# A four-layer network on one core: how the modes' parts of a long-convolution kernel are split and loaded, and where the first layer's norm is computed

## The chip, the cores and the metric

The kernel runs on one core of one Trainium2 chip. A core has five engines that run side by side, each with its own queue of instructions: TensorE (PE: products; PEld: the loading of their weights), VectorE (DVE), ScalarE (ACT), GpSimd (POOL), and SyncE (SP), which here issues nearly all of the DMAs. The metric is the device time of one execution in microseconds (us). Times are compared by the median of several runs; the profile is of one execution.

## The reference

The input is a matrix x of 2048 positions by 512 channels. Four residual layers follow one another, A, B, A, B, and each takes a layer norm over the channels first:

```
x = x + A(layernorm(x));  x = x + B(layernorm(x))      # twice
A(x) = irfft2(rfft2(x) * (w_r + i w_i))                # 2048 x 512, a spectral filter
B(u) = irfft(rfft(u, 4096) * rfft(K, 4096))[:2048] + u * D_skip
K[d, l] = 2 Re sum_n C[d, n] exp(A[d, n] dt[d] l)      # 128 modes n for each channel d
A[d, n] = -exp(log_A_real) + i A_imag;  C = (C_real + i C_imag) dt;  dt = exp(log_dt)
```

K, the kernel in time, does not depend on x; both B layers use the same one. The norm subtracts the mean of a row and divides by the root of its variance.

## The kernel before

Transforms are done as products with tables of cosines and sines, in steps that TensorE can do. Three strands matter here.

**The first layer A** has three stages. *Spread* (`layer_a.spread`, 16 steps) loads rows of x, takes their norm and transforms along the positions. *Middle* (18 steps) transforms along the channels, weighs with w and goes back. *End* (`end`, 19 steps) consists of `fold` (lines 565 to 590: products, a copy on ScalarE, an addition and a subtraction on VectorE, and additions on GpSimd that give the tile wv) and, three steps later, of `rows_back` (592 to 614): a product gives 128x512 values of one row per partition, the residual row hr is loaded from x, VectorE adds the product to it (601), and the sum is stored to DRAM (603), where the next layer reads it. When a group of rows is complete (`LN`, here groups of 4, 4, 4, 2, 1, 1 rows), `layer_norm_stats` computes two numbers for each row, scale and offset, into `norms`: statistics per row (339), their aggregation (340), and a chain of small VectorE operations per group, an inverse square root by three Newton steps (345 to 362).

**The modes of the second layer's K.** `kernel_parts` computes five numbers per mode and channel into the tile val (called V; raw, tmp and val are its working tiles): logarithm and phase of the start, decay, and two phases. `kernel_parts` is a generator: each `yield` ends one of its ten steps, which are put in between the first layer's spread steps (1123). At the end (769 to 775) it splits the 128x2560 values of all four blocks of channels into three bf16 parts that add up to them: a cast on ScalarE (771), a subtraction on VectorE (773), and a store to the DRAM tensor parts for each part.

**The kernel in time** (`kernel_time`) runs 32 units, eight for each block of channels, in groups of four. For every second unit, `chunk` (788) loads the parts of 32 rows into the tile th, with six DMAs of 48 partitions: a slot holds two of the five numbers, one in partitions 0 to 47 and the other in 48 to 95. `grow` (804) makes magnitudes (products with the table kb at 825, exponentials, a GpSimd product); `bend`, `sine`, `cosine`, `terms` (857 to 859) and `total` (870) make the sums over the modes. Their steps are put in between the steps of the first layer's middle and end and of the second layer, by fixed shares (`FILL`).

The program is written as one list of steps, interleaved as described. A scheduler places each instruction into its engine's queue ahead of time, by the order of the program and a model of when inputs and buffers are ready; on the chip every engine then runs its own queue in that order. Tiles of one tag share a fixed number of buffers, and a new tile waits for the last user of the old one. In the first layer the tags o, f, wv and junk all draw on the seven buffers of w, and hr on the four of wt. The phase k, with kb and th, reuses the space of phase m, with raw, val, tmp and hp (the bf16 parts).

Of the kernel before, what the change touches and what calls it, by code (L numbers as in the profile page):

```python
# [32 lines left out]
WT = 4  # L33
WA = 7
LN = '444211'
PK = 2
PV = 1
# [22 lines left out]
KP = 0  # L60
S1 = 0
S2 = 0
S3 = 0
# [183 lines left out]
class Net:  # L247
# [135 lines left out]
    def layer_a(self, w, x=None, src=None, dst=None):  # L383
# [178 lines left out]
        done = []  # L562
        sizes = [int(c) for c in reversed(LN)]

# [27 lines left out]
        def rows_back(n2):  # L592
            old = row(n2, self.sb("hr", [512])) if x is None else x[:, n2]
            p = self.ps("p3", [512])
            nc.tensor.matmul(p, vs["tat"][:, n2], vs.pop(n2), start=True, stop=True)
            if not done:
                norm["sums"] = self.sb("lsum", [4], 2)
            if S2 if x is None else S3:
                self.add_up(old, old, p, norm["sums"][:, len(done):len(done) + 1])
            else:  # L600
                nc.vector.tensor_add(old, old, p)
            if x is None:
                self.dma("D")(dst[:, n2], old)
            done.append(old)
            if len(done) == sizes[-1]:
                sizes.pop()
                n = len(done)
                nr = self.layer_norm_stats(done, newton=x is None or NW[2] == "1", sums=norm["sums"][:, :n] if (S2 if x is None else S3) else None,
                                           nr=self.norms[:, :, n2 - n + 1:n2 + 1] if x is None else None)
                if x is not None:  # L610
                    for i in range(n):
                        nc.scalar.activation(self.xn[:, n2 - n + 1 + i], done[i], ACT.Identity,
                                             bias=nr[:, 0, i:i + 1], scale=nr[:, 1, i:i + 1])
                done.clear()
# [78 lines left out]
    def kernel_parts(self, kin, log_dt, parts, blks, *tags):  # L693
# [50 lines left out]
        nc.scalar.activation(mn, mn, ACT.Ln, bias=1.0)  # L744
        L = V[:, :, 2]
        D.scalar_tensor_tensor(L, e, LN2, mx, op0=ALU.mult, op1=ALU.add)
# [11 lines left out]
        D.tensor_scalar_mul(V[:, :, 0], im, -0.5)  # L758
        for c, o in ((64.0, V[:, :, 3]), (32.0, u)):
# [4 lines left out]
        D.scalar_tensor_tensor(V[:, :, 4], ph, 1 / (2 * PI), u, op0=ALU.mult, op1=ALU.add)  # L764
        yield
        self.exp(re, S[:, 2:5])
        D.scalar_tensor_tensor(V[:, :, 1], re, -1.0, dtb, op0=ALU.mult, op1=ALU.mult)
        yield
        for part in range(3):
            H = self.sb(tags[3], [n, 5, 128], dt=BF)  # L770
            nc.scalar.copy(H, V)
            if part < 2:
                D.tensor_sub(V, V, H)
            nc.sync.dma_start(parts[blks.start:blks.stop, :, part].rearrange("b q r n -> r b q n"), H)
            yield

    def kernel_time(self, parts, kt, units, group):
# [10 lines left out]
        def chunk(blk, ch):  # L788
            th = self.sb("th", [3, 2, 128], dt=BF, rows=96)
            for slot, q in enumerate((0, 1, 3)):  # L790
                for i in range(2):
                    self.dma("C")(th[48 * i:48 * i + 48, slot],
                                      parts[blk, q + i, :, 32 * ch:32 * ch + 32].rearrange("p (c h) n -> p c h n", h=2))
            state["th"] = th
# [9 lines left out]
        def grow(i):  # L804
# [9 lines left out]
            mag = self.sb("mag", [3, 512])  # L814
            for k, (slot, c) in enumerate(((0, RM), (0, RN), (1, RP))):
                if k == 1 and RNP[i % len(RNP)] != "a":
# [7 lines left out]
                p = self.ps("pk", [512])  # L824
                nc.tensor.matmul(p, th[:, slot, h], c, start=True, stop=True)
                ordered(mag[:, k], p, ACT.Exp)
            live[i] = mag, th

        def bend(i, j):
# [4 lines left out]
            p = self.ps("pk", [2, 256])  # L834
            nc.tensor.matmul(p[:, 0], th[:, 0, h], KQ[:, e], start=True, stop=False, skip_group_check=True)
            nc.tensor.matmul(p[:, 1], th[:, 2, h], KP[:, e], start=False, stop=False, skip_group_check=True)
            p = p.rearrange("p k d -> p (k d)")
# [389 lines left out]
```

## Time and profile before

| what | value |
|---|---|
| runs | 787.24, 789.84 and 782.07 us (median 787.24) |
| span of the profiled execution, first to last instruction | 781.1 us |
| its own time | not listed apart from the runs; it is at least the span |
| instructions | 18929 |
| VectorE busy | 649.3 us (83% of the span) |
| TensorE busy, products | 627.7 us (80%) |
| ScalarE busy | 428.1 us (55%) |
| GpSimd busy | 404.9 us (52%) |
| granted TensorE clock, mean | 0.934 of full speed |
| moved by DMA | 80.64 MB, mean 103 GB/s |

A row of the profile's groups reads: line, engine, operation, output tile <- input tiles, shapes and count, then busy time and mean duration of one (ns), then the idle time of the engine just before them and what ended most of it. A row of one line's instructions gives durations as min/median/max in ns and the first and last start in us. A row of the timeline gives start, duration, engine, line, operation and tiles. Busy times can overlap a wait for another engine's port, and a busy TensorE is not one at its peak.

### The profile page before, as it was taken

How to read it: one execution, taken by the hardware profiler on the slowest of the kernel's cores; microseconds unless marked ns; L12 is line 12 of the kernel's file. 1: busy time of each engine (PE TensorE's matmuls, PEld its weight loads, DVE VectorE, ACT ScalarE, POOL GpSimd, SP SyncE). 2: the span in 40 equal slices, each digit the busy share in tenths (PEclk: the TensorE clock that was granted, in tenths of full speed). 3: DMA queues.
4: the chain of work that ended last, by engine and by line, in shares of the span. 5: the costliest groups of instructions: out<-in, count | busy, mean ns of one | idle time of the engine just before them, and what ended most of it. 6: DMA issues, size and time to landing. Idle time of an engine off the chain costs nothing. (4 is left out here: it accounts for less than half of the span.)

```text
span 781.1 us, 18929 instructions
## 1 busy us (share of the span) xinstructions
PE 627.7 (80%) x7248; PEld 443.5 (57%) x7248; DVE 649.3 (83%) x1301; ACT 428.1 (55%) x919; POOL 404.9 (52%) x596
## 2 busy tenths in 40 slices
PE   3447888897867977998889887874899896989986
PEld 2336666665534543656365656654777663566766
DVE  7998748979998999769996997878578696889992
ACT  3433778854748765887568834323756336242312
POOL 3675876764825245721657266281055572475760
PEclk9998899999979997999989999997999999799998
DMA  8300552344546503452325539422133114234513
GB/s 311 128 0 1 129 138 56 110 75 151 114 167 184 137 9 64 124 145 82 51 68 117 192 55 257 141 95 69 55 82 83 28 28 136 70 95 120 154 29 83
DMA packets 144923, 80.64 MB, mean 103 GB/s; under 512 B 78561, under 2 KB 124513, under 8 KB 143937
## 3 DMA queue, kind: packets, MB, share of 16 engines
q1 hardware_dynamic: 144576, 78.90, 36.2%
q8 instruction: 58, 0.95, 0.5%
q0 software_dynamic: 256, 0.52, 0.4%
q14 instruction: 33, 0.26, 0.1%
HBM read 54.89 MB, written 25.03 MB: 102 GB/s over the span
## 5 line engine op out<-in xcount | busy, mean ns | idle before, releaser
L974 POOL TENSOR_TENSOR u<-wb,wb 64x512 f32<-64x512 f32 x90 | 129.2, 1436 | 85.2 <-DVE wb L962 75.9
L316 PE MATMUL p<-z,mb 128*64 128x512 f32 (+2 forms) x480 | 102.0, 535 | 8.3 <-DVE wb L962 5.4
L870 PE MATMUL pv<-qp 128*64 128x128 f32 x1024 | 78.9, 295 | 11.4 <-DVE qp L859 6.9
L859 DVE TENSOR_TENSOR qp<-qp,mag 128x1024 f32<-128x1024 f32 x64 | 83.8, 1317 | 1.0
L962 DVE TENSOR_TENSOR wb<-p,kk 128x512 f32<-128x512 f32 x128 | 80.6, 674 | 4.7 <-PE p L316 4.6
L870 PEld LDWEIGHTS pv<-qp 128*64 128x64 f32 x1024 | 62.0, 147 | 38.8 <-ACT stage L878 10.2
L648 ACT COPY z<-p 128x512 f32<-128x512 f32 x96 | 51.4, 597 | 58.1 <-PE p L316 43.7
L316 PE MATMUL p<-mb,u 128*64 128x64 f32 x2048 | 72.9, 235 | 10.6 <-DVE u L974 4.5
L316 PEld LDWEIGHTS p<-mb,u 128*64 128x64 f32 x2048 | 70.7, 150 | 18.7 <-issue 11.3
L857 DVE SCALAR_TENSOR_TENSOR qp<-qp,mag 128x256 f32<-128x256 f32 x128 | 64.8, 523 | 13.6 <-ACT qp L800 13.3
L654 DVE STREAM_TRANSPOSE z<-z 128x512 f32<-128x512 f32 x96 | 58.5, 673 | 18.0 <-ACT z L648 18.0
L527 DVE TENSOR_TENSOR w<-wt,p 128x514 f32<-128x514 f32 x64 | 42.6, 686 | 33.3 <-PE p L316 18.6
L1086 POOL TENSOR_SCALAR w<-w,norms 128x128 f32<-128x128 f32 x64 | 40.5, 647 | 51.9 <-DMA w<-h 28.3
L532 POOL TENSOR_TENSOR w<-w,w 64x257 f32<-64x257 f32 x48 | 40.1, 835 | 50.3 <-DVE w L527 46.2
L456 PE MATMUL p<-w,w 128*128 128x128 f32 x128 | 32.0, 429 | 40.8 <-DVE w L449 30.8
L987 ACT COPY u<-p 128x512 f32<-128x512 f32 x64 | 37.6, 590 | 43.8 <-PE p L316 43.8
L316 PEld LDWEIGHTS p<-z,mb 128*64 128x64 f32 x480 | 34.2, 140 | 37.0 <-issue 20.2
L456 PEld LDWEIGHTS p<-w,w 128*128 128x128 f32 x128 | 27.8, 318 | 44.7 <-issue 24.8
L800 ACT ACTIVATE kf<-pk 128x512 f32<-128x512 f32 x64 | 38.9, 608 | 24.1 <-PE pk L839 23.6
L316 PE MATMUL p<-t,w 64*64 64x128 f32 x1024 | 43.3, 290 | 5.8 <-issue 2.6
L974 DVE TENSOR_TENSOR u<-wb,wb 64x512 f32<-64x512 f32 x38 | 46.9, 1234 | 0.5
L800 ACT ACTIVATE qp<-kf,half 128x512 f32<-128x512 f32 x64 | 47.2, 737 | 0.1
(200 smaller groups left out, 1495.3 us busy)
## 6 DMA issues: line engine op xcount, KB each, us to landing
wt<-in_w SPq DMA_DIRECT2D x32, 257.0 KB
kf<-kk SPq DMA_DIRECT2D x32, 256.0 KB
kk<-kf SPq DMA_DIRECT2D x32, 256.0 KB
u<-in_x SPq DMA_DIRECT2D x16, 256.0 KB
hr<-in_x SPq DMA_DIRECT2D x16, 256.0 KB
kt<-stage SPq DMA_DIRECT2D x32, 128.0 KB
h<-hr SPq DMA_DIRECT2D x16, 256.0 KB
w<-kt SPq DMA_DIRECT2D x32, 128.0 KB
```

Source lines behind the costliest of these rows:

```text
L316: last = self.nc.tensor.matmul(out, weights, data, start=not more, stop=True, skip_group_check=True).ins
L456: nc.tensor.matmul(p[:, b], xf[:, b], t, start=True, stop=True)
L527: nc.vector.tensor_mul(m[pl], W, px[:, None, :].to_broadcast([128, 2, 257]))
L648: nc.scalar.copy(tiles["z"][:, :, :, b, m:m + 2].rearrange("p u j m r -> p (u j) (m r)"), ps[b].rearrange("p u j m r -> p (u j) (m r)"))
L654: nc.vector.transpose(tiles["zt"][:, u:u + 8].rearrange("p u j d -> p (u j d)"), tiles["z"][:, u:u + 8].rearrange("p u j b m r -> p (u j b ...
L800: last["x"] = nc.scalar.activation(*a, **k).ins
L857: nc.vector.scalar_tensor_tensor(QP[:, c, 0], QP[:, c, 1, :, ::-1], -1.0 if c else 1.0, m[:, 0], op0=ALU.mult, op1=ALU.mult)
L859: nc.vector.tensor_mul(t, t, mag[:, None, 1:3, 256 * j:256 * j + 256].to_broadcast([128, 2, 2, 256]))
L870: nc.tensor.matmul(p[64 * t:64 * t + 64, g], QP[:, c, 2, d:d + 2].rearrange("p s a -> p (s a)"), QP[:, c, 0:2, d:d + 2].rearrange("p k s b ...
L962: nc.vector.tensor_mul(split(m[c, pl], "du", [32, 16]), by_channel(p), split(k[c], "du", [32, 16]))
L974: self.added = e[0].tensor_sub(y[0:64], v[0, 0], v[1, 1]), e[1].tensor_add(y[64:128], v[0, 1], v[1, 0])
L1086: (self.nc.gpsimd if XNE[k] == "g" else self.nc.vector).tensor_scalar(t[:, k], t[:, k], scale, bias, op0=ALU.mult, op1=ALU.add)
```

## The change

Two parts of the kernel change.

*The modes' parts.* The five numbers are stored in another order, so that three neighbouring ones (0 to 2, and 2 to 4) form what th needs in its two halves; number 2 is stored twice. The split runs for block 0 first and then for blocks 1 to 3 together (`BLKS`): six casts, four subtractions and twelve stores in place of three, two and three. `kernel_parts` now has 13 steps, all of which are put in between the same spread steps. DRAM rows are 384 bf16 values long. `chunk` loads th with one DMA of 96 partitions, 768 contiguous values each; th has the slot as its second index.

*The first layer's norm.* `S2` is 1: the residual addition also leaves the row's sum (`add_up`, a tensor_tensor_reduce on VectorE). `layer_norm_stats` turns the sums into means with one small operation, squares each row with the mean as bias on ScalarE and lets that sum up (lines 324 to 332), and scales the result; then the same chain follows. Groups have 6, 6 and 4 rows (`LN1`). The rows hr get eight buffers of their own instead of sharing the four of wt. The second A layer keeps `LN` and its statistics.

```diff
+BLKS = [slice(0, 1), slice(1, 4)]
+LN1 = '664'
-S2 = 0
+S2 = 1
-        return [step] * 10
+        return [step] * 13
...
-        sizes = [int(c) for c in reversed(LN)]
+        sizes = [int(c) for c in reversed(LN1 if x is None else LN)]
...
-                norm["sums"] = self.sb("lsum", [4], 2)
+                norm["sums"] = self.sb("lsum", [8], 2)
...
-        for part in range(3):
-            H = self.sb(tags[3], [n, 5, 128], dt=BF)
-            nc.scalar.copy(H, V)
-            if part < 2:
-                D.tensor_sub(V, V, H)
-            nc.sync.dma_start(parts[blks.start:blks.stop, :, part].rearrange("b q r n -> r b q n"), H)
-            yield
+        for bs in BLKS:
+            v = V[:, bs]
+            for part in range(3):
+                H = self.sb(tags[3], [bs.stop - bs.start, 5, 128], dt=BF)
+                nc.scalar.copy(H, v)
+                if part < 2:
+                    D.tensor_sub(v, v, H)
+                for i in range(2):
+                    nc.sync.dma_start(parts[bs, i, part].rearrange("b r s n -> r b (s n)"),
+                                      H[:, :, 2 * i:2 * i + 3].rearrange("p b s n -> p b (s n)"))
+                yield
...
-            th = self.sb("th", [3, 2, 128], dt=BF, rows=96)
-            for slot, q in enumerate((0, 1, 3)):
-                for i in range(2):
-                    self.dma("C")(th[48 * i:48 * i + 48, slot],
-                                      parts[blk, q + i, :, 32 * ch:32 * ch + 32].rearrange("p (c h) n -> p c h n", h=2))
+            th = self.sb("th", [2, 3, 128], dt=BF, rows=96)
+            self.dma("C")(th, parts[blk, :, :, 32 * ch:32 * ch + 32].rearrange("i p (c h) s n -> (i p) c (h s n)", h=2))
...
-    parts = net.dram.tile([4, 5, 3, 128, 128], mybir.dt.bfloat16, name="parts")
+    parts = net.dram.tile([4, 2, 3, 128, 3, 128], mybir.dt.bfloat16, name="parts")
...
-                    net.phase("a", x=(32768, 1), ta=(8192, 1), ca=(6912, 1), u=(16384, 2), w=(2056, WA), wt=(2056, WT), hr="wt",
+                    net.phase("a", x=(32768, 1), ta=(8192, 1), ca=(6912, 1), u=(16384, 2), w=(2056, WA), wt=(2056, WT), hr=(2048, 8),
                               wv="w", junk="w"):
```

The other lines of the diff put the five numbers into their new places.

More of the change, by code (lines that the diff above doesn't have):

```diff
@@ L744, in kernel_parts @@
         nc.scalar.activation(mn, mn, ACT.Ln, bias=1.0)
-        L = V[:, :, 2]
+        L = V[:, :, 4]
         D.scalar_tensor_tensor(L, e, LN2, mx, op0=ALU.mult, op1=ALU.add)
@@ L758, in kernel_parts @@
         D.tensor_scalar_mul(V[:, :, 0], im, -0.5)
-        for c, o in ((64.0, V[:, :, 3]), (32.0, u)):
+        for c, o in ((64.0, V[:, :, 1]), (32.0, u)):
             D.tensor_scalar_mul(lm, im, c)
@@ L763, in kernel_parts @@
         D.tensor_add(u, u, V[:, :, 0])
-        D.scalar_tensor_tensor(V[:, :, 4], ph, 1 / (2 * PI), u, op0=ALU.mult, op1=ALU.add)
+        D.scalar_tensor_tensor(V[:, :, 3], ph, 1 / (2 * PI), u, op0=ALU.mult, op1=ALU.add)
         yield
         self.exp(re, S[:, 2:5])
-        D.scalar_tensor_tensor(V[:, :, 1], re, -1.0, dtb, op0=ALU.mult, op1=ALU.mult)
+        D.scalar_tensor_tensor(V[:, :, 2], re, -1.0, dtb, op0=ALU.mult, op1=ALU.mult)
         yield
-        for part in range(3):
-            H = self.sb(tags[3], [n, 5, 128], dt=BF)
-            nc.scalar.copy(H, V)
-            if part < 2:
-                D.tensor_sub(V, V, H)
-            nc.sync.dma_start(parts[blks.start:blks.stop, :, part].rearrange("b q r n -> r b q n"), H)
-            yield
+        for bs in BLKS:
[9 more added lines that the diff above has]
+                yield
     def kernel_time(self, parts, kt, units, group):
@@ L814, in grow @@
             mag = self.sb("mag", [3, 512])
-            for k, (slot, c) in enumerate(((0, RM), (0, RN), (1, RP))):
+            for k, (slot, c) in enumerate(((0, RM), (0, RN), (2, RP))):
                 if k == 1 and RNP[i % len(RNP)] != "a":
@@ L824, in grow @@
                 p = self.ps("pk", [512])
-                nc.tensor.matmul(p, th[:, slot, h], c, start=True, stop=True)
+                nc.tensor.matmul(p, th[:, h, slot], c, start=True, stop=True)
                 ordered(mag[:, k], p, ACT.Exp)
@@ L834, in bend @@
             p = self.ps("pk", [2, 256])
-            nc.tensor.matmul(p[:, 0], th[:, 0, h], KQ[:, e], start=True, stop=False, skip_group_check=True)
-            nc.tensor.matmul(p[:, 1], th[:, 2, h], KP[:, e], start=False, stop=False, skip_group_check=True)
+            nc.tensor.matmul(p[:, 0], th[:, h, 0], KQ[:, e], start=True, stop=False, skip_group_check=True)
+            nc.tensor.matmul(p[:, 1], th[:, h, 1], KP[:, e], start=False, stop=False, skip_group_check=True)
             p = p.rearrange("p k d -> p (k d)")
```

## The prediction

> **What bounds the kernel now.** I read a table by stage first, not the page's busy shares, because the two edits sit in two stages: the parts of the modes are made until 96 us, and the first layer's norm is taken between 157 and 248 us. The columns of the table are PE, PEld, DVE, ACT and POOL busy, the granted clock, the DMA share and GB/s.
>
> ```profile
> 76.00:107.00 31.00, 25.11 (x168) 18.95 (x169) 19.97 (x26) 22.34 (x47) 23.89 (x50) 0.89 0.60 133
> 107.00:157.00 50.00, 44.37 (x354) 32.35 (x353) 38.37 (x56) 43.55 (x99) 33.86 (x69) 0.93 0.29 86
> 157.00:245.00 88.00, 72.43 (x535) 46.77 (x538) 82.01 (x199) 52.07 (x104) 44.15 (x65) 0.90 0.47 128
> 245.00:463.00 218.00, 186.47 (x2469) 118.09 (x2458) 188.78 (x337) 155.28 (x297) 102.13 (x124) 0.93 0.41 102
> ```
>
> From 157 to 245 us, where the first layer folds its result back and takes its norm, VectorE is busy 82.0 of 88 us (93%), TensorE 72.4, ScalarE 52.1. From 76 to 107 us VectorE works 20.0 of 31 us and nothing is full. So a microsecond of VectorE work is worth most in the norm's stage, and an earlier start of anything new is worth most before 107 us.
>
> The second view is one line of the code, L825: the first product of each unit of the kernel in time. Units go in groups of four, two products each, so a row of eight is the start of one group; the last row is the end of all of them.
>
> ```profile
> L825 PE MATMUL pk<-kb,th x8: 376/386/631, 107.6 to 117.4; 96*128 96x512 bf16 x8
> L825 PE MATMUL pk<-kb,th x8: 376/376/390, 147.4 to 156.7; 96*128 96x512 bf16 x8
> L825 PE MATMUL pk<-kb,th x8: 376/379/390, 188.6 to 203.5; 96*128 96x512 bf16 x8
> L825 PE MATMUL pk<-kb,th x8: 376/389/631, 235.6 to 246.7; 96*128 96x512 bf16 x8
> L825 PE MATMUL pk<-kb,th x8: 376/379/390, 277.8 to 287.2; 96*128 96x512 bf16 x8
> L870 PE MATMUL pv<-qp x1024: 272/273/477, 130.1 to 458.9; 128*64 128x128 f32 x171
> ```
>
> The groups begin 39.8, 41.2, 47.0 and 42.2 us apart, and the last four take (458.9 - 277.8) / 4 = 45.3 us each. They run side by side with every other stage until 459 us, and the frequency products of the last block need all of them. So the kernel in time is a thread that paces the first 460 us: what it gains at its start or in a slow group is gained by all behind it.
>
> **Part 1: the modes' parts and their loads.** Now the values are ready at 75.6 us, are cast and subtracted for all four blocks together, and leave in three stores; then come the loads.
>
> ```profile
> 74.90 0.69 DVE L764 SCALAR_TENSOR_TENSOR val<-tmp 128x512 f32<-128x512 f32 x1
> 78.17 2.33 ACT L771 CAST hp<-val 128x2560 bf16<-128x2560 f32 x1
> 96.07 0.38 SPq L774 DMA_DIRECT2D parts<-hp  x1
> 100.76 8.91 SPq L792 DMA_DIRECT2D th<-parts  x12
> 102.41 0.73 POOL L808 DMA_DIRECT2D kb<-in_kb  x1
> ...
> L773 DVE TENSOR_TENSOR val<-val,hp 128x2560 f32<-128x2560 f32 x2 | 5.6, 2822 | 0.0
> ...
> PE pk L825 <- DMA kb<-in_kb: 1.7, 1, 1.7
> ```
>
> The first cast starts at 78.17 and the last store is issued at 96.07: 17.9 us, of which 3 x 2.33 + 2 x 2.82 = 12.6 us are work and 5.3 us are waits behind the first layer's own copies. The loads go out 4.7 us after the last store and the first product starts 6.8 us after the first load, held up at the end by the table of constants kb (1.7 us).
>
> After the change the same elements go through six casts and four subtractions. Block 0 is a quarter of each: 0.6 us a cast and 0.7 us a subtraction, so its chain is 3 x 0.6 + 2 x 0.7 = 3.2 us of work and could be stored by about 85 us. But the buffers of the loads lie where the values lay (the pools of the two phases reuse the same space), and the values are freed by the last cast of blocks 1 to 3, not of block 0. So I don't take 85 us as the start. Ten steps instead of five carry the same 12.6 us of work, some 0.2 us more each for starting (what the smallest operations take, L352 below), hence about 19 us from first cast to last. In their favour: the last store's landing (4.7 us) no longer stands before the first load; one load per chunk issues in one instruction instead of six (0.74 us each by the row of twelve, so 3.7 us less per chunk); and the seven steps that make the values come at 7/13 of the way through the first layer's spread instead of 7/10, which I put at 2 us, an estimate: two of its twelve steps move behind them. Sum: last cast ends at 96 + 1 - 2 = 95, load issued and landed by 98, constants by 101 since their issue sits on POOL's queue behind the first layer's work: the first product at about 101.5, **6 us earlier** than 107.6. The ends are 0 (the constants do not move) and -20 (everything moves with block 0).
>
> SP's queue gets 12 stores instead of 3 (9 x 0.38 = 3.4 us more, in a stretch where its queue only carries weights) and 16 loads instead of 96:
>
> ```profile
> L792 SPq DMA_DIRECT2D th<-parts x96: 682/684/857, 100.8 to 406.8; - x96
> ...
> 233.25 4.39 SPq L792 DMA_DIRECT2D th<-parts  x6
> 237.68 5.27 SPq L909 DMA_DIRECT2D w<-kt  x8
> 243.00 1.70 SPq L1080 DMA_DIRECT2D w<-h  x3
> ```
>
> That is 96 x 0.684 = 65.7 us of SP's queue against 16 x 0.684 = 10.9 us. It matters where something urgent stands behind: at 233.25 a chunk's loads delay w<-kt and then w<-h, the inputs of the next stage, by 3.7 us. VectorE is full there, so I cost this at nothing, with -4 as the other end.
>
> **Part 2: the norm.** These are VectorE's groups in the stage (count | busy us, mean ns), then the times of the residual addition.
>
> ```profile
> L339 DVE BATCH_NORM_STATS2 bst<-hr 128x6 f32<-128x512 f32 x16 | 10.9, 679 | 0.0
> ...
> L357 DVE TENSOR_TENSOR lnt<-lnt,lnv 128x4 f32<-128x4 f32 (+2 forms) x18 | 4.5, 261 | 0.0
> L356 DVE SCALAR_TENSOR_TENSOR lnt<-lnr 128x4 f32<-128x4 f32 (+2 forms) x18 | 4.3, 254 | 0.0
> L340 DVE BATCH_NORM_AGGREGATE bmv<-bst 128x2 f32<-128x6 f32 x16 | 2.4, 162 | 0.0
> L358 DVE SCALAR_TENSOR_TENSOR lnr<-lnt,lnr 128x4 f32<-128x4 f32 (+2 forms) x12 | 2.4, 207 | 0.0
> L358 DVE SCALAR_TENSOR_TENSOR norms<-lnt,lnr 128x4 f32<-128x4 f32 (+2 forms) x6 | 1.2, 192 | 0.0
> L345 DVE TENSOR_SCALAR lnv<-bmv 128x4 f32<-128x4 f32 (+2 forms) x6 | 1.1, 184 | 0.0
> ...
> L601 DVE TENSOR_TENSOR hr<-hr,p x16: 647/672/687, 164.4 to 229.2; 128x512 f32<-128x512 f32 x16
> ```
>
> Removed: statistics 10.9 and aggregation 2.4 = 13.3 us. The chain behind them is 13 small operations per group (L345, L349, L350, nine of L356 to L358, L362); the rows shown are 60 of the 78 and sum to 13.5 us, 0.22 each, so 78 cost 17 us. With three groups and two more operations each (the mean, the scaling of the squares) it is 45 x 0.22 = 10 us: 7 us less. Added: the addition keeps a sum. The trace has no such form; below it lies the plain addition (0.67 us, nothing added), above it the same plus one small operation to write the sum (0.16 to 0.22 us). I take 0.2, so 16 x 0.2 = 3 us. Net: VectorE loses 13.3 + 7 - 3 = **17 us** of 82.
>
> The Trainium skill, "VectorE: DVE Perf Modes", section "Two Vector instructions with no wait between them", speaks on the side of the upper end: an operation that also writes its accumulator is two instructions, the main one and an accumulator read. By it the 3 us stand; without it they would be 0; no row here shows either.
>
> ScalarE gets 16 squares of 128x512 with a pointer as bias and a sum.
>
> ```profile
> L800 ACT ACTIVATE qp<-kf,half 128x512 f32<-128x512 f32 x16 | 11.7, 729 | 0.0
> ...
> L800 ACT ACT_TABLE_LOAD x4 | 5.1, 1283 | 0.1
> ...
> L352 ACT ACTIVATE lnt<-lnv x15: 188/205/223, 5.4 to 661.7; 128x4 f32<-128x4 f32 x10, 128x2 f32<-128x2 f32 x3, 128x1 f32<-128x1 f32 x2
> ```
>
> The nearest row with a pointer as bias takes 0.729; writing the sum costs between nothing and one small operation (0.205): 0.93 at most, 16 x 0.93 = 15 us. ScalarE goes from 52 to 67 of 88. If squares needed another table than the exponentials and sines, two loads a group would add 3 x 2 x 1.28 = 7.7; I take 0 and keep that end.
>
> The Trainium skill, "ScalarE: Activation LUTs", section "Rules for kernel authors", speaks against this edit: additions and products belong on VectorE, which is faster per element. Row by row this trace agrees barely (0.68 for the statistics, 0.73 for the square). By the rule the part would lose 15 - 13 = 2 us if both engines were equally full; they are not (93% against 59%).
>
> How much of 17 us comes back? With 65 us left VectorE is no longer the fullest: TensorE has 72.4 and ScalarE 67. If the stage fills TensorE as it now fills VectorE, 72.4 / 0.93 = 78 us, 10 less. ScalarE is in the way of the thread (its exponentials and sines queue behind the squares, up to 6 x 0.93 = 5.6 us in a burst), so I take **6 us**; the ends are 0 and -16. The thread agrees: its two groups within this stage take 41.2 + 47.0 = 88.2 us, against 2 x 40 in the stage before: 8 to gain.
>
> Waits added: with groups of four, each row's statistics follow its own addition; now the squares of a row wait for the mean of six. Eight buffers hold the rows, so the load of row 8 waits on SP for row 0's square, and behind it stand stores of rows and th loads; VectorE's addition of row 8 waits in front of the thread's products. Two rows of slack at 65 / 16 = 4 us a row cover 8 us; the square, the load and the queue take about 0.9 x 2 + 3 + 1. I charge 1 us for each of the two boundaries: **+2**. The last group has four squares and 15 small operations, 4 x 0.93 + 15 x 0.22 = 7 us behind the last addition (229.9), done at 237 if not queued, before the first normed row is wanted:
>
> ```profile
> L1086 POOL TENSOR_SCALAR w<-w,norms x16: 446/452/1487, 246.7 to 257.0; 128x128 f32<-128x128 f32 x16
> ```
>
> That costs nothing; exposed it would be +7. **Sum: -6 - 6 + 2 = -10 us.**
>
> **The rivals.** *Both parts in full:* VectorE's 17 us come back, and the start moves by more than 6 because block 0 alone decides: -16 - 6 + 0 = -22. For it: the thread's groups follow one another. Against: TensorE at 82% is next.
>
> *Absorbed:* the groups keep 39 to 47 us whatever VectorE does (45 after 278 us too, where it is at 87%), so its saving becomes idle time, and the constants' load does not come earlier: -6 x 0.5 + 0 + 2 = about -1. For it: the pace hardly follows the load. Against: the slowest early group is the one in the fullest stage.
>
> *Slower: the squares' bursts.* The squares write into the same seven buffers as the fold's own tiles. Where a burst of six takes six of seven, the fold stops for 6 x 0.93 = 5.6 us at each of two boundaries, and the last group's 7 us are exposed: 11 + 7 = 18, less 6 for the start and 2 of the norm: +10. It decides if the fold cannot run on into its free buffers when a burst begins. For it: each engine runs its instructions in an order fixed beforehand, and ScalarE's holds the thread's too. Against: VectorE then has the thread's products to do.
>
> **How the numbers follow.** The profiled span is 781.1 us; the runs go from 782.07 to 789.84, so this execution is like the fastest of them, and the median, 787.24, lies 6 above the span. I carry the -10 to the median: 777. The cases: forecast (771 to 783) 0.45; both in full (765) 0.12; absorbed (786) 0.22; bursts (797) 0.21. The range leaves out the outer half of the last two ends: 766 to 796. One per cent, 7.9 us, is about what this kernel's measurement can tell from no change. Below 779.3: three quarters of the forecast and all of the full case, 0.46; above 795.1: most of the bursts, 0.19; the rest 0.35.
>
> **What the changed profile would show.** L825's first row at 100 to 103 us; two statistics groups gone from the stage, 16 squares in their place at 0.73 to 0.95 us; VectorE near 65 us in it, and the fourth group of L825 some 12 us earlier than 235.6. Wrong would be: the first product still at 107, then the constants or the freed space decide; VectorE idle behind PE or ACT in the norm's stage, then it was no longer the bound; additions waiting for loads of hr at rows 6 and 12, then the bursts decide.

## The result and the profile after

The changed kernel took 794.65 us (median of 18 runs, 788.67 to 807.06); the kernel before, on the same chip, 786.84 us (18 runs, 777.92 to 791.06). The ratio is 1.0116 [1.0089, 1.0142]: **slower by 1.2%**, where 777 was forecast. Two of the 18 runs of the changed kernel are in a slower state of the chip, and ratios leave such runs out here and below, and a ratio is not the quotient of the medians beside it. The profiled span is 792.9 us against 781.1. A run is about 1.8 us longer than its span (794.68 against 792.9 for the changed kernel), so the traced execution of the kernel before took some 783 us, 4 less than its median, while that of the changed kernel lies at its median: a part of the 11.8 us between the two spans is this choice of execution.

The table by stage of the changed kernel, columns as in the prediction:

```profile
76.00:107.00 31.00, 22.67 (x161) 16.85 (x162) 18.76 (x25) 22.71 (x48) 21.70 (x45) 0.97 0.56 157
107.00:157.00 50.00, 44.44 (x379) 32.73 (x380) 41.09 (x59) 43.58 (x102) 33.42 (x70) 0.97 0.19 58
157.00:245.00 88.00, 73.66 (x622) 48.56 (x620) 71.91 (x173) 64.38 (x140) 51.39 (x77) 0.96 0.53 139
245.00:463.00 218.00, 178.47 (x2225) 109.72 (x2222) 179.75 (x299) 151.49 (x287) 93.68 (x110) 0.91 0.37 92
```

In the norm's stage VectorE fell from 82.0 to 71.9 us and ScalarE rose from 52.1 to 64.4. Behind it, from 245 to 463 us, VectorE is busy 9.0 us less than before (179.75 against 188.78), though the change takes no work out of this stretch: VectorE waits there, and some of the work comes after 463 us.

The first products of the groups of the kernel in time (L825 is now L829), and its end; below them the sixth group of the kernel before:

```profile
L829 PE MATMUL pk<-kb,th x8: 376/381/634, 106.9 to 116.0; 96*128 96x512 bf16 x8
...
L829 PE MATMUL pk<-kb,th x8: 376/379/382, 195.5 to 211.2; 96*128 96x512 bf16 x8
L829 PE MATMUL pk<-kb,th x8: 376/390/390, 237.0 to 249.8; 96*128 96x512 bf16 x8
L829 PE MATMUL pk<-kb,th x8: 376/378/389, 282.7 to 291.3; 96*128 96x512 bf16 x8
L829 PE MATMUL pk<-kb,th x8: 377/384/390, 334.5 to 342.4; 96*128 96x512 bf16 x8
...
L874 PE MATMUL pv<-qp x1024: 272/273/477, 127.5 to 468.8; 128*64 128x128 f32 x171
```

```profile
L825 PE MATMUL pk<-kb,th x8: 376/378/390, 324.1 to 332.3; 96*128 96x512 bf16 x8
```

The first starts 0.7 us earlier than before (107.6), the third 6.9 later, the fourth 1.4, the fifth 4.9, the sixth 10.4 later (334.5 against 324.1), the last product 9.9 later. The norm's stage gives its loss back by the fourth group; the lasting loss arises between 237 and 335 us, behind the stage that was changed. From the end of the kernel in time to the end of the program it is 324.1 us, before it was 322.2: the thread sets the time, as the prediction had it, and it became longer.

How that looks on the busiest engine: one row for the stretch from the first product of the kernel in time to its last, before and after.

```profile
107.60:458.90 351.30, 299.16 (x3268) 194.62 (x3267) 305.05 (x583) 249.19 (x494) 179.59 (x256) 0.92 0.41 107
```

```profile
106.90:468.80 361.90, 301.95 (x3290) 195.48 (x3291) 297.12 (x537) 261.58 (x531) 184.03 (x262) 0.92 0.38 97
```

Before: 351.3 us, VectorE busy 305.1, so idle 46.2. After: 361.9, busy 297.1, idle 64.8. VectorE has 7.9 us less work and 18.6 us more idle time; the difference is the 10.6 us by which the thread is longer. The view of waits says what VectorE waited for in these stretches (total us, times, longest), before and then after:

```profile
DVE qp L857 <- ACT qp L800: 13.3, 17, 2.5
DVE z L654 <- ACT z L648: 8.3, 4, 3.8
...
DVE w L527 <- POOL w L534: 6.1, 1, 6.1
DVE w L582 <- ACT w L579: 5.5, 2, 4.4
DVE w L527 <- PE p L316: 1.8, 1, 1.8
DVE kw L838 <- PE pk L836: 1.6, 3, 0.7
```

```profile
DVE qp L861 <- ACT qp L804: 20.8, 20, 4.0
DVE z L657 <- ACT z L651: 12.5, 5, 5.6
DVE kw L842 <- PE pk L840: 11.7, 10, 3.4
DVE w L530 <- PE p L319: 8.0, 3, 5.5
```

The rows qp and kw are the thread's own hand-overs: a unit goes PE, VectorE (kw), PE, ScalarE, VectorE (qp). They grow together from 14.9 to 32.5 us, which is 17.6 of the 18.6 us of added idle time. The rows z and w belong to the stages beside the thread; z grows by 4.2 us, and the waits for w shrink from 13.4 in the three rows before to 8.0.

The groups of the norm's stage (157 to 245 us) that are new or changed, count | busy us, mean ns:

```profile
L332 ACT ACTIVATE junk<-hr,lnm 128x512 f32<-128x512 f32 x16 | 11.3, 716 | 3.6 <-DVE lnm L330 3.6
...
L371 DVE CUSTOM_DVE_ANT_0 hr<-hr,p 128x512 f32<-128x512 f32 x16 | 10.8, 677 | 3.6 <-ACT kf L804 2.3 <-PE p L598 1.3
...
L359 DVE SCALAR_TENSOR_TENSOR lnt<-lnr 128x6 f32<-128x6 f32 (+1 forms) x9 | 2.3, 253 | 0.0
L360 DVE TENSOR_TENSOR lnt<-lnt,lnv 128x6 f32<-128x6 f32 (+1 forms) x9 | 2.0, 223 | 0.0
...
L371 DVE DVE_READ_ACCUMULATOR2_ANT lsum<- 128x1 f32 x16 | 1.3, 78 | 0.0
```

The rows of the start, in order of time (part 1):

```profile
76.30 0.74 ACT L776 CAST hp<-val 128x640 bf16<-128x640 f32 x1
...
94.70 1.79 ACT L776 CAST hp<-val 128x1920 bf16<-128x1920 f32 x1
...
98.26 1.67 SPq L797 DMA_DIRECT2D th<-parts  x2
...
101.20 0.73 POOL L812 DMA_DIRECT2D kb<-in_kb  x1
```

### The profile page after: what moved, and what is told of

It is laid out like the page before. It is cut to its first block, busy times and chain, and to the rows that moved or that the text cites. A ratio compares the mean times of both kernels' runs of the same rounds, so it can differ in the third digit from the quotient of the medians.

```text
span 792.9 us, 18782 instructions
## 1 busy us (share of the span) xinstructions
PE 628.4 (79%) x7248; PEld 441.4 (56%) x7248; DVE 636.7 (80%) x1254; ACT 439.2 (55%) x954; POOL 408.9 (52%) x596
## 5 line engine op out<-in xcount | busy, mean ns | idle before, releaser
L978 POOL TENSOR_TENSOR u<-wb,wb 64x512 f32<-64x512 f32 x90 | 130.0, 1444 | 120.6 <-DVE wb L966 109.2
L319 PE MATMUL p<-z,mb 128*64 128x512 f32 (+1 forms) x480 | 102.6, 538 | 11.4 <-DVE wb L966 7.4
L874 PE MATMUL pv<-qp 128*64 128x128 f32 x1024 | 80.7, 302 | 12.3 <-DVE qp L863 5.3
L874 PEld LDWEIGHTS pv<-qp 128*64 128x64 f32 x1024 | 63.2, 150 | 33.4 <-ACT stage L882 10.4
L1090 POOL TENSOR_SCALAR w<-w,norms 128x128 f32<-128x128 f32 x64 | 42.8, 682 | 55.9 <-DMA w<-h 55.2
L535 POOL TENSOR_TENSOR w<-w,w 64x257 f32<-64x257 f32 x48 | 35.8, 745 | 54.0 <-DVE w L530 44.2
L459 PEld LDWEIGHTS p<-w,w 128*128 128x128 f32 x128 | 27.7, 319 | 47.7 <-issue 25.0
L842 DVE TENSOR_SCALAR kw<-pk 128x512 bf16<-128x512 f32 x64 | 43.3, 681 | 11.9 <-PE pk L840 11.7
L548 PE MATMUL p<-ca,w 128*128 128x128 f32 x256 | 40.4, 288 | 9.2 <-POOL w L536 4.1
```

Of the source, the lines that this page charges most:

```text
L319: last = self.nc.tensor.matmul(out, weights, data, start=not more, stop=True, skip_group_check=True).ins
L459: nc.tensor.matmul(p[:, b], xf[:, b], t, start=True, stop=True)
L842: nc.vector.tensor_scalar(whole, p, MAGIC, -MAGIC, op0=ALU.add, op1=ALU.add)
L874: nc.tensor.matmul(p[64 * t:64 * t + 64, g], QP[:, c, 2, d:d + 2].rearrange("p s a -> p (s a)"), QP[:, c, 0:2, d:d + 2].rearrange("p k s b ...
L978: self.added = e[0].tensor_sub(y[0:64], v[0, 0], v[1, 1]), e[1].tensor_add(y[64:128], v[0, 1], v[1, 0])
L1090: (self.nc.gpsimd if XNE[k] == "g" else self.nc.vector).tensor_scalar(t[:, k], t[:, k], scale, bias, op0=ALU.mult, op1=ALU.add)
```

## The experiments

Each ratio is against runs of the kernel before on the same chip. "Thread" is the kernel in time, from its first product to its last; idle is that length less VectorE's busy time in it, by the one row of the table by stage as above; rest is from the thread's end to the end of the span. These columns come from one execution of each kernel. For most it lies within 3 us of the median of the runs, but for before some 4 us under it, for e9 9.4, e11 8.3 and e17 4.9 under it, and for e10 4.4 above it.

| run | ratio [95%] | thread, us | length | VectorE busy | idle | rest |
|---|---|---|---|---|---|---|
| before | 1 | 107.6-458.9 | 351.3 | 305.1 | 46.2 | 322.2 |
| after | 1.0116 [1.0089, 1.0142] | 106.9-468.8 | 361.9 | 297.1 | 64.8 | 324.1 |
| e1 norm only | 0.9979 [0.9942, 1.0016] | 108.4-461.2 | 352.8 | 290.6 | 62.2 | 323.0 |
| e2 parts only | 1.0069 [1.0032, 1.0106] | 107.2-467.6 | 360.4 | 305.3 | 55.1 | 324.8 |
| e3 three groups | 1.0147 [1.0098, 1.0195] | 108.8-472.0 | 363.2 | 300.1 | 63.1 | 321.8 |
| e4 squares, six groups | 1.0091 [1.0053, 1.0128] | 107.1-466.2 | 359.1 | 298.0 | 61.1 | 325.6 |
| e5 spacing only | 1.0077 [1.0039, 1.0115] | 104.1-469.0 | 364.9 | 305.8 | 59.1 | 322.0 |
| e6 layout only | 1.0111 [1.0048, 1.0173] | 105.5-471.2 | 365.7 | 307.5 | 58.2 | 324.3 |
| e7 split only | 1.0136 [1.0052, 1.0221] | 108.2-476.6 | 368.4 | 306.8 | 61.6 | 323.5 |
| e8 norm and layout | 1.0108 [1.0070, 1.0146] | 107.0-469.5 | 362.5 | 292.1 | 70.4 | 323.4 |
| e9 rows' own buffers | 1.0011 [0.9970, 1.0052] | 107.6-460.3 | 352.7 | 306.5 | 46.2 | 316.2 |
| e10 short statistics | 1.0056 [1.0015, 1.0097] | 110.0-465.3 | 355.3 | 296.2 | 59.1 | 325.9 |
| e11 double statistics | 1.0246 [1.0139, 1.0352] | 107.2-480.1 | 372.9 | 313.2 | 59.7 | 317.0 |
| e12 change, thread first | 1.0214 [1.0139, 1.0290] | 108.2-479.6 | 371.4 | 294.0 | 77.4 | 321.4 |
| e13 norm, spacing | 1.0142 [1.0068, 1.0216] | 104.6-473.0 | 368.4 | 296.1 | 72.3 | 322.7 |
| e14 before, thread first | 1.0284 [1.0213, 1.0355] | 109.3-482.5 | 373.2 | 304.4 | 68.8 | 322.6 |
| e15 norm, thread first | 1.0380 [1.0305, 1.0455] | 108.7-483.8 | 375.1 | 288.2 | 86.9 | 333.1 |
| e16 before, later rows | 0.9975 [0.9938, 1.0011] | 108.1-459.0 | 350.9 | 303.2 | 47.7 | 323.6 |
| e17 change, later rows | 1.0020 [0.9978, 1.0062] | 106.7-464.2 | 357.5 | 292.6 | 64.9 | 319.4 |
| e18 norm, later rows | 1.0062 [1.0019, 1.0105] | 109.2-469.4 | 360.2 | 292.9 | 67.3 | 320.1 |

The last column is the first finding: in 19 of 20 kernels the program ends 316 to 326 us behind the thread (e15: 333). The two lowest, 316.2 and 317.0, are e9 and e11, whose traced executions were the fastest against their medians. So what is to be explained first is the thread's length, 351 to 375 us.

**One part alone.** e1 takes the norm's edits only, e2 the modes' parts only (the rest of the diff). e3 and e4 cut the norm's part in two: both have e1's `hr=(2048, 8)`; e3 the three groups with the old statistics, e4 the squares with the old groups.

```diff
 # e1, against before; e2 has the other hunks of the change
+LN1 = '664'
-S2 = 0
+S2 = 1
...
-hr="wt",
+hr=(2048, 8),
 # e3, against e1
-S2 = 1
+S2 = 0
 # e4, against e1
-LN1 = '664'
+LN1 = '444211'
```

> Only the norm's part of the change: sums from the addition, squares on ScalarE, groups of 6, 6 and 4 rows, hr with buffers of its own; the modes' parts as before. Theory N (the squares stand in ScalarE's queue in front of the thread of the kernel in time): all of the loss, 9 to 10 us, ratio 1.012, with the third group of L825 some 6 us later than before. Theory P (the earlier and smaller pieces of the modes' parts slow the first layer's spread and middle): ratio 0.99 to 1.00, since VectorE loses about 15 us of work in its fullest stage.

> Only the modes' parts: block 0 split first, 13 steps, one load per chunk; the norm as before. Theory N: faster by 0 to 5 us (0.994 to 1.000), since the loads' issue shrinks and nothing else changes. Theory P: slower by 6 to 12 us (1.008 to 1.015); the last spread product some 3 us later than 72.3 and the first back product later than 80.3.

> Three groups of 6, 6 and 4 rows and hr with eight buffers, but the rows' statistics on VectorE as before (no squares, no sums); the modes' parts as before. If the grouping makes the loss: 1.010 or more. If the squares on ScalarE make it: 0.99 to 1.00, since three chains of small operations are gone from VectorE (some 7 us).

> Sums from the addition and squares on ScalarE, but in the old groups of 4, 4, 4, 2, 1 and 1 rows, hr with eight buffers; the modes' parts as before. If bursts of six squares make the loss, it shrinks to a half or less here (1.000 to 1.005); if it is ScalarE's load as such, it stays at 1.010.

Measured: 784.65, 792.81, 797.07 and 791.58 us, against 786.34. The norm's part alone costs nothing; its two halves, each of which does less of it, cost 1.5% and 0.9%. No sum of costs of parts gives that. The groups of at most four squares in e4 don't help, and the groups of six in e1 cost nothing, so the bursts aren't the price. Theory N, which put the whole loss on the norm, falls with e1; e2 lies between the ranges of both theories, just under that of P.

**Spacing, layout, split.** e5 is the kernel before with one number changed; the generator is then exhausted after its tenth step, and nothing is added. e6 has the new layout and the single loads with one block of four; e7 the split with the old layout; e8 is e6 with the new norm.

```diff
 # e5
-        return [step] * 10
+        return [step] * 13
 # e6, against e2; e8, against after
-BLKS = [slice(0, 1), slice(1, 4)]
+BLKS = [slice(0, 4)]
-        return [step] * 13
+        return [step] * 10
 # e7, against before, with [step] * 13
+        for bs in [slice(0, 1), slice(1, 4)]:
+            v = V[:, bs]
...
+                nc.sync.dma_start(parts[bs, :, part].rearrange("b q r n -> r b q n"), H)
```

> The kernel before, with 13 in place of 10 steps set apart for making the modes' parts: no operation, transfer or byte is added or removed, the seven steps that make the values come earlier in the spread and the last three places are empty. Theory S (spacing and the order that follows from it): the loss of the parts alone, 5.5 us, sits here already: about 792 us where the kernel before has 786.3, with the loss between the fifth and sixth group of the kernel in time (277.8 to 324.1 us before). Theory D (split): nothing without the split itself, 786. Theory L (layout and single load): 786. Theory O (any new order of the queues scatters by several us, of either sign): off by 3 us or more from 786 on either side, and from the parts alone as well.

> The new order of the five numbers, the doubled number and one load per chunk, with the split left for all four blocks together in three casts and six stores, and ten steps as before. Theory L: the loss is here, about 792. Theory S: 786, or a few us less since 80 loads of 0.68 us leave SP's queue. Theory D: 786. Theory O: off by 3 us or more on either side of 786. First product of the kernel in time at 106 to 108 us by all of them, as it waits for the constants.

> Block 0 split first and then blocks 1 to 3, in 13 steps, but with the old layout: six stores, and six loads per chunk. Theory D: the loss is here, about 792. Theory S: also 792, since its 13 steps are those of the spacing run. Theory L: 786. Theory O: off by 3 us or more on either side, and away from the spacing run, though the steps stand at the same places.

> The changed kernel with the split undone (three casts, ten steps) and the rest kept: the norm from sums and the single loads. If the split or the spacing is what costs (theories D, S), this gives the norm's part alone, 784.7, or up to 4 us less by the shorter SP queue: 781 to 785, faster than both kernels. Theory L: 790 to 795, as the changed kernel. Theory O: no forecast better than 786 with some 6 us either way.

Measured: 793.92, 796.63, 800.06 and 794.29 us, against 787.18. All four are slower, and e5 tells why this isn't a price of the split: with not one operation more or less than the kernel before, and a thread that starts 3.5 us earlier, it loses what e2 loses. Its row for the thread:

```profile
104.10:469.00 364.90, 306.49 (x3314) 199.63 (x3316) 305.77 (x588) 252.50 (x505) 185.14 (x269) 0.93 0.40 104
```

VectorE's busy time is that of before (305.8 against 305.1), its idle time 59.1 us against 46.2. What differs is the order: the scheduler, which places the instructions by its own model of times, put some 200 of VectorE's 1,301 instructions in another place of the sequence (counted in the two traces). Theories D and L, which expected e6 or e7 at 786, fall (L had e8 right), and so does S on e6, which has the old spacing and loses more.

**Order held, order changed.** e9 changes only SP's queue: on the four computing engines every instruction stays in its place. e10 takes work from VectorE (the statistics leave out three quarters of each row, so its result is not that of the reference), e11 adds work, e12 is the changed kernel with the thread first.

```diff
 # e9
-wt=(2056, WT), hr="wt",
+wt=(2056, WT), hr=(2048, 8),
 # e10, in the first layer only; in both, the second layer A sets self.second
-                    nc.vector.bn_stats(st, row)
+                    nc.vector.bn_stats(st, row[:, 0:128] if newton and row.shape[-1] == 512 and not hasattr(self, 'second') else row)
 # e11, in the first layer only
                     nc.vector.bn_stats(st, row)
+                    if newton and not hasattr(self, 'second'):
+                        nc.vector.bn_stats(st, row)
 # e12, against after
-KP = 0
+KP = 50
```

> The kernel before with the residual rows hr in eight buffers of their own: the queues of TensorE, VectorE, ScalarE and GpSimd keep the order of the kernel before, instruction by instruction; only SP's queue changes (the loads of hr stand earlier). Theory O (the order of the queues makes the difference): same as before, within 3 us of 787, and VectorE's waits while the kernel in time runs stay near the 44.6 us of the kernel before. Rival H (hr's own buffers and the changed SP queue cost): 791 to 793, as the run with three groups and statistics kept, 797, would then owe it.

> The kernel before, where the first layer's statistics read only the first 128 of a row's 512 numbers (the other three quarters are left out): about 16 x 0.5 = 8 us of VectorE's 82 in the norm's stage go, and nothing is added on any engine. Theory V (a microsecond of VectorE in that stage is worth about a third, as the prediction had it): 3 us faster, 784; at most 8, 779. Theory O: the smaller price makes another order, so no gain that can be forecast: 787 to 795, VectorE's busy time 8 us lower and its waits while the kernel in time runs at 55 to 63 us in place of 44.6.

> The kernel before, with the first layer's statistics taken twice: 16 x 0.68 = 10.9 us more on VectorE in the stage where it has 82 of 88. Theory V: 3.6 to 11 us slower, 791 to 798, and further from before than the short statistics are on their side. Theory O: slower too, but by the same 4 to 10 us as the edits that add no work at all; the two can't be told apart by the time alone, but by VectorE's busy time and waits while the kernel in time runs: V has the waits stay near 44.6 us and the busy time rise by 11; O has the waits near 60.

> The changed kernel with the kernel in time's steps given priority over all other steps in the scheduler (KP = 50 in place of 0): the same work in another order. If the kernel in time paces the first 460 us (theory O and the prediction say so), its end, 468.8 us in the changed kernel, comes earlier, by 5 to 20 us, and the time falls as much: 775 to 790. Rival W (the other stages set the time, and the kernel in time only goes with them): its end comes earlier, but what follows no longer takes 324 us behind it, and the time stays at 793 or rises.

Measured: 787.63, 788.84, 807.19 and 801.62 us, against 788.46. The rows of e9, e10 and e11:

```profile
107.60:460.30 352.70, 298.54 (x3266) 193.07 (x3267) 306.51 (x584) 248.81 (x494) 177.19 (x256) 0.93 0.39 101
```

```profile
110.00:465.30 355.30, 297.24 (x3266) 194.62 (x3267) 296.20 (x582) 249.71 (x493) 175.93 (x251) 0.92 0.40 106
```

```profile
107.20:480.10 372.90, 305.61 (x3268) 198.40 (x3267) 313.19 (x600) 249.37 (x493) 186.50 (x255) 0.90 0.39 101
```

With the order held, time and idle time (46.2) are those of before; hr's buffers cost nothing, and e3's loss isn't theirs. In e10 VectorE is busy 8.9 us less in the thread, nothing is added, and the kernel is still not faster than before (1.0056): idle time 59.1. Between e10 and e11, whose idle times agree within 0.6 us, 17.0 us of VectorE's work go with 17.6 us of thread, and the runs are 1.9% apart, about 15 us. That looks like a microsecond for a microsecond, but it is one pair whose two kernels also differ in order, and orders alone make differences of that size (below), so it isn't shown. e11 missed the ranges of both of its theories, which ended at 798. A new order can cost 13 us of idle time in the traces (e5), as much as the new norm takes off VectorE; in the time it is 0.8%, 6 us, since e5's thread starts 3.5 us earlier and the traced execution of before lies under its median. e12 is a miss of both theories it names: priority for the thread in the scheduler made the thread longer (371.4 us, idle 77.4); being planned first did not make the thread end first.

**What the work is worth apart from the order.** Pairs whose only difference is the norm (or the whole change), under three more orders: 13 places (e13, pair of e5), thread first (e14, e15, beside e12), and rows going back one step later (e16, e17, e18).

```diff
 # e13, against e1
-        return [step] * 10
+        return [step] * 13
 # e14 against before, e15 against e1
-KP = 0
+KP = 50
 # e16 against before, e17 against after, e18 against e1
-LAGE = 3
+LAGE = 4
```

> The norm's part alone, with the 13 places of the spacing run: the pair of the spacing run (793.9, 1.0077 of before) with the new norm as the only difference in work. Theory O (the order of the queues adds some 5 to 13 us to every re-planned kernel; the norm's own worth is a few us in its favour): 786 to 792. Theory Z (the norm's own worth is nothing, the norm alone was a lucky order): 791 to 797.

> The work of the kernel before, with priority for the kernel in time (KP = 50): the pair of the changed kernel with priority (801.6, 1.0214). Theory O: another order of the same work is slower than before again, 792 to 806, with VectorE's waits while the kernel in time runs at 55 us or more against 44.6. If the changed kernel's own work costs 1.2%, as the two medians say, then 801.6 less 9, 792; if its work is worth a few us in its favour, 801 to 806.

> The norm's part alone, with the same priority for the kernel in time. Theory O with a norm worth a few us: 3 to 7 us faster than the kernel before with that priority. Theory Z: no gain against it; over the pairs the differences average to nothing.

> The work of the kernel before, with the first layer's rows going back four steps behind their fold instead of three (LAGE = 4): again no operation added or removed, another order. Theory O: 790 to 800, VectorE's waits while the kernel in time runs at 55 us or more. If the order of the kernel before were nothing special, the time would lie on either side of 787, say 780 to 794.

> The changed kernel with rows going back four steps behind their fold (LAGE = 4): its pair is the kernel before with the same lag (784.0, 0.9975). If the change's own work costs 1.2%, 793 to 794. If it is worth nothing and the order decides, anywhere from 780 to 800; together with the two other pairs (changed against before 1.0116; changed with priority against before with priority 1.0214 / 1.0284 = 0.993) the differences would then not have one sign.

> The norm's part alone with the same lag; pairs so far (norm alone against before -0.2%, with the spacing +0.65%, with priority +0.96%, the change against its parts alone +0.47%, with the layout -0.03%) give +0.4% on average. If the new norm is worth nothing by itself or costs that, 784 to 790; if theory O's few microseconds in its favour hold, 777 to 781, faster than both kernels.

Measured: e13 to e16 797.77, 808.32, 815.89 and 784.03 us against 787.43; e17 and e18 790.25 and 790.74 against 785.18. Theory O fell in one half: e16 is a new order that costs nothing (0.9975), so the order of before isn't alone in being good. It held in the other: the same work under four orders (that of before and e9, e5, e14, e16) runs from 0.9975 to 1.0284. How many instructions move doesn't tell the cost: of VectorE's 1,301 some 145 are in another place in e16, which loses nothing, and some 120 in e14, which loses 2.8%. e13 and e14 came out 1 to 2 us above the ranges of their theories; e17 and, within 1 us, e18 are where a norm that is worth nothing would put them.

The norm's part, as quotients of ratios: e1 to before 0.998, after to e2 1.005, e8 to e6 1.000, e13 to e5 1.006, e15 to e14 1.009, e18 to e16 1.009; mean 1.004. The 4 us that the prediction gave the norm (6 less 2) would be 0.995, and none of the six goes below 0.998; the gain that theory O gave it isn't there either. In the same six pairs VectorE's busy time falls by 14.4, 8.2, 15.4, 9.7, 16.2 and 10.3 us, 12.4 on average, and its idle time grows by 16.0, 9.7, 12.2, 13.2, 18.1 and 19.6, 14.8 on average. **What is taken off VectorE comes back on VectorE as waiting.** That is bookkeeping, as an engine in a thread that gets no shorter must be idle where it isn't busy; what the pairs show is that the thread gets 2.4 us longer on average, and shorter in one of six (e8, by 3.2). One of the pairs in full, e16 and then e18, with the thread's row and its first waits:

```profile
108.10:459.00 350.90, 296.54 (x3266) 190.14 (x3267) 303.20 (x582) 249.51 (x494) 180.94 (x253) 0.93 0.41 107
```

```profile
DVE kw L838 <- PE pk L836: 12.0, 8, 4.5
DVE qp L857 <- ACT qp L800: 9.8, 12, 2.8
```

```profile
109.20:469.40 360.20, 304.74 (x3266) 195.34 (x3267) 292.90 (x534) 260.30 (x525) 179.84 (x254) 0.91 0.38 98
```

```profile
DVE qp L858 <- ACT qp L801: 21.4, 18, 4.4
DVE kw L839 <- PE pk L837: 10.9, 8, 3.9
```

VectorE has 10.3 us less to do, ScalarE 10.8 more, and VectorE's products of the thread wait 11.6 us longer for ScalarE. That wait (qp on ACT) grows in all six pairs, by 1.4 to 11.6 us. It can't be put down to ScalarE's new work alone: in e5, where no engine has more to do, it grows by 8.3 us (13.3 to 21.6). The whole change gives 1.0116 (against before), 0.993 (e12 to e14) and 1.005 (e17 to e16): no one sign, on average 0.3%.

So the 1.2% of the changed kernel lies within what orders alone do here, and the runs give the change's own work no cost or gain that stands clear of that. What stays open is which exchanges in the order cost the time. A kernel with the order of before and less work on VectorE wasn't tried: the scheduler prices the instructions, and cheaper statistics alone (e10) already gave another order. Nor does any run beat the kernel before beyond its interval.

## Why the prediction was wrong, step by step

- **What bounds the kernel.** That the thread paces the first 460 us and that all behind it goes with it held, to within 10 us, in all runs but e15. That VectorE's busy share marks where a microsecond is worth most did not: in six pairs, with VectorE 12.4 us less busy on average, the thread got 2.4 us longer, and what grew in all six were the thread's waits for ScalarE.
- **First product 6 us earlier** failed: 0.7. The cast and the load came as worked out (last cast ended at 96.5, forecast 95; load issued at 98.3, forecast issued and landed by 98). The mis-sized term is the constants, put at 101: 101.20 is when kb's load was issued, and the product started 5.7 us later (106.9). Before it was 102.41 and 107.6, 5.2 us; the landing stood in the rows quoted and was left out of the sum. TensorE stood idle for kb in front of the first product for 2.2 us (1.7 before).
- **VectorE loses 17 us of 82** was right as a sum of durations and wrong as busy time. Added up by instruction, as the prediction did, VectorE's durations fall by 17.6 us over the program (731.2 to 713.6, in the traces). But instructions overlap on the engine: in the stage before, 96.5 us of durations are 82.0 us of busy time, and the forecast took a sum of the one from the other. Busy time fell by 12.6 us over the whole span (649.3 to 636.7) and by 10.1 in the stage, into which more of the thread's work moved (TensorE has 622 rows there against 535). The sums cost 0.08 us each (the accumulator's read) and not 0.2, the small operations of the groups 0.16 to 0.44 by kind and not 0.22 throughout. By the Trainium skill, "VectorE: DVE Perf Modes", section "Two Vector instructions with no wait between them", an operation with an accumulator output is two instructions; the trace agrees, with 16 rows of 0.677 us and 16 of 0.078.
- **ScalarE +15 us**: 16 x (0.716 + 0.19) = 14.5, as forecast, and four table loads in the stage as before. But it was costed as room on an engine at 59%, and the thread's sines and exponentials, which stand in that queue, came into the sum only as the reason to take 6 instead of 10.
- **6 of the 17 come back** is the step that failed most: on average over the six pairs none did, as the idle time grew by 2.4 us more than the work shrank. With 0.7 in place of the first 6, 0 in place of this one and the +2 kept, the sum would be about +1. The other 8 us of the measured 9 have no term in the prediction: 5 of them come with the modes' parts alone (e2, 0.7%), whose thread is 9 us longer with the same VectorE work; e5's is 14 us longer with no change of work at all.
- **Waits of six-row groups, +2**, and the **bursts** rival: a burst did come (six squares between 209.2 and 214.4 us, after a wait of 3.6 us for the mean), but e1 has the same groups and costs nothing, and e4 without them costs 0.9%. The sign named for it, additions waiting for loads of hr, does not appear among VectorE's waits after the change.
- **The fourth group 12 us earlier** than 235.6: 237.0, while VectorE had 71.9 us there and not 65.
- **The rivals.** By its number the bursts case, 797, is nearest to 794.65, but that is luck, as its mechanism cost nothing. By the mechanism "absorbed", 786, is nearest: the saving became idle time, as it said. The case of both parts in full says that the start moves by more than 6 us, and its sum takes 6. What none of the cases held is that the queues are planned anew after an edit (e9 kept the order), and that this alone moves the time by 1% and more.

## What to carry to other kernels

Where a scheduler places the instructions by a model, run an edit that changes no work (here one number for the spacing) before crediting or blaming a real one: its scatter, 0.9975 to 1.0284 here, is the resolution of any single comparison of two plans. Judge an edit by pairs under several orders, and by busy and idle time of the engine over the thread that sets the end, not by busy time alone. In this kernel VectorE, busy 87% of a chain of hand-overs, gave nothing back on average when 12 us of its work went to another link of the chain; whether it would with the order held was not tried.

## What the runs showed of the hardware that was not expected

In these traces, stretches in which TensorE is little busy are followed by some in which its granted clock is half. In the table by stage, the stretch from 290 to 335 us, where the thread lost most, before and then after:

```profile
290.00:335.00 45.00, 37.74 (x468) 24.04 (x469) 39.54 (x57) 30.44 (x59) 29.55 (x30) 0.85 0.36 85
```

```profile
290.00:335.00 45.00, 31.74 (x346) 21.53 (x346) 35.87 (x49) 23.16 (x44) 18.87 (x17) 0.70 0.32 72
```

The granted clock is 0.70 against 0.85. Cut finer, in the changed kernel it is 1.00 from 287 to 291 us and 0.50 from 293 to 299, behind two microseconds with TensorE busy for 0.68; again 0.50 from 303 to 313 behind four with 1.30, and 0.50 from 320 to 327 behind seven with 3.40. The kernel before shows it too: 0.61 from 299 to 303 and 0.50 from 303 to 308, behind three microseconds with 0.38. In the timeline of the changed kernel the same 16 products take 1.97 us in place of 1.09:

```profile
287.88 1.09 PE L874 MATMUL pv<-qp 128*64 128x128 f32 x16
...
293.44 1.97 PE L874 MATMUL pv<-qp 128*64 128x128 f32 x16 [1.76 <-DVE qp L863]
```

The Trainium skill, "TensorE: Matmul & The Clock Gate", section "What's actually happening", has two states, a full clock and half of it when TensorE has been idle for a window; the factor of 1.8 between these rows and the granted 0.50 agree, though the longest idle time just ahead of this drop is 1.76 us, and the kernel before has one of 1.74 (at 290.5 us) without a drop. So a wait can lengthen the next products. It does not by itself explain the longer thread: over the thread as a whole the granted clock is 0.92 before and after.
